# Folding the projection instead of its input, four products at the last frequencies, and an earlier transpose of the next pair in the first four pairs

## The chip, the cores and the metric

The kernel runs on one core of a Trainium2 chip. The metric is the device time of one execution in microseconds (us); lower is better. The core has five engines, each with its own instruction queue that is worked off in order: TensorE (PE; its weight loads are listed apart as PEld), VectorE (DVE), ScalarE (ACT), GpSimd (POOL) and SyncE (SP), which here only issues transfers. PE writes its results to PSUM; DVE and ACT read them there. Engines wait for one another on semaphores.

## The reference

Attention with 4 batches, 8 heads, 768 positions and 64 columns a head; some heads attend to all earlier positions, the others only to the first 4 and the last 64. The result, laid side by side over the heads (768 x 512 for each batch), goes through a gated long convolution:

```python
a = np.exp(scores - max);  a = a / a.sum(-1)          # causal, or causal and (sink or window)
x = (a @ v) laid out as [B, S, 512]
proj = x @ w_proj                                      # 512 -> 3 * 512
x1, x2, x3 = proj in three parts
x2_conv = irfft(rfft(x2, axis=1) * rfft(filter_fft, axis=0), axis=1)
y = x1 * x2_conv * x3
out = y @ w_out
```

## The kernel before

**Attention.** The heads are taken in pairs: 16 pairs n = 0 to 15, four for each batch. For each pair q and k are loaded, cast to bf16 on POOL (`emit_cast`), and transposed to `qkT` (`emit_prep`): for n < 6 by PE, then copied out of PSUM by DVE (q half, L131) and ACT (k half, L133); from n = 6 on by a transposing transfer on SP's queue (L135). The causal blocks of scores are cut into six chunks, two for each third of a pair; `emit_chunks(st, third)` multiplies into PSUM (L318) and takes the exponential on ACT (L325) into `pT`; `emit_masking` multiplies the near blocks by the mask on DVE (L332). `emit_values` (L341, PE) multiplies by v with a column of ones appended, `emit_norm` divides by that column's sum on DVE (L351, L352), and `emit_turn` transposes the result into `xT`: by PE with a DVE copy (L359, L361) for n < 6 and for the last pair of a batch, else by a transfer on SP's queue. POOL also casts v and multiplies it by a mask (`v_aug`, `v_far`).

**Convolution.** The transform over 768 positions is split by even and odd frequencies. For that the sum and the difference of the two halves of the sequence are needed: `emit_fold` makes them from `xT` into `xf`, two operations for each pair, on POOL (128x384 each, L370 and L371), and on DVE for the last pair of a batch. `moe` is a generator for one batch, one `yield` a step: three steps of `x2` (the projection of `xf`, PE L380, then ACT L383); four steps of `X` (the transform by the matrix `G`, PE L254, then ACT): two groups t = 0, 1 with cosine rows and sine rows of 128 frequencies each, and for the last frequencies (t = 2) a tile with 64 cosine and 64 sine rows and once more the same with the rows swapped (`Xs`); the products with the filter's spectrum (`HA`, `HB`) on DVE, `P = X*HA + Xs*HB` (L398, L400, L401); eight steps of `x1` and `x3` (L411, L418, L420); four steps of the inverse transform by `Gi` (six products of 128x384 in each, L427) with ACT and DVE behind it (L430 to L434); three steps of the output product (L440, L443) with a transfer out. `G` is made at the start; `emit_matrix` (POOL) finishes it and `Gi` is its transpose. `setup_steps` transforms the filter in the same manner, also as a generator, in pairs 2 to 4.

**What sets the order.** In pairs 0 to 4 all engines run in the order in which the code is written. From pair 5 on (`MANUAL`) only POOL and SP do; PE, DVE and ACT are put in order by the scheduler at build time, from the same program. `gate_step` takes one step of the generators; a pair from n = 4 on has five such places, so 20 a batch, while `moe` has 22 steps. What is left after pair 15 runs in the tail. PSUM has four buffers of two banks (`bank_pair`) for everything.

## Time and profile before

| | us |
|---|---|
| median of three runs | 253.22 |
| lowest, highest of them | 250.37, 485.48 |
| the profiled execution | 249.91 |
| its span, first to last instruction | 248.2 |

The span has three stages that can be told apart in the trace: a start (0 to about 64 us: setting up, pairs 0 to 4, the filter's transform), a middle (64 to about 200 us: pairs 5 to 15 with the convolution of the batch before woven in) and a tail (200 us to the end: the rest of the third batch's convolution and the whole fourth). PE is busy in 80% of the span, DVE in 66%, ACT in 61%, POOL in 39%.

### The profile page before, as it was taken

The numbers are of one execution on the slowest core, as the hardware profiler recorded it, in microseconds if no ns is written. First come the engines' busy times: TensorE is split into PE (matmuls) and PEld (weight loads), VectorE is DVE, ScalarE is ACT, GpSimd is POOL, SyncE is SP. The second block draws the span as 40 slices with busy tenths as digits, with TensorE's granted clock in tenths as the row PEclk, the third lists the DMA queues.
The fourth block names the chain that finished last, engine by engine and source line by source line (L and its number), as shares of the span: only waits on it lengthen the run. The fifth ranks groups of instructions, "written<-read, shape, count | busy, mean of one in ns | idle before, by whom it ended". The sixth has DMA issues, their size and how long they took to land.

```text
span 248.2 us, 4240 instructions
## 1 busy us (share of the span) xinstructions
PE 197.9 (80%) x1704; PEld 105.0 (42%) x1718; DVE 165.0 (66%) x246; ACT 152.4 (61%) x186; POOL 96.1 (39%) x125
## 2 busy tenths in 40 slices
PE   1533758594899799959997997699899989999880
PEld 0312546252254446523544644353446543455520
DVE  6999588779348964992359749941696593085730
ACT  4956458364479576736897767549896433672431
POOL 5596578772027373470307758420330300000000
PEclk9999995799599999979999999999999999999997
DMA  7999999991031999972899999539211001500015
GB/s 195 301 287 249 288 195 212 198 234 29 0 65 29 213 162 180 219 124 53 262 209 177 216 202 220 98 118 188 45 32 34 4 0 57 196 3 0 0 39 215
DMA packets 89843, 34.42 MB, mean 139 GB/s; under 512 B 80864, under 2 KB 86752, under 8 KB 89824
## 3 DMA queue, kind: packets, MB, share of 16 engines
q1 hardware_dynamic: 86928, 31.28, 57.9%
q0 software_dynamic: 2896, 2.88, 7.1%
q8 instruction: 13, 0.21, 0.4%
q14 instruction: 6, 0.05, 0.1%
HBM read 24.65 MB, written 6.29 MB: 125 GB/s over the span
## 4 chain that ended last, share of the span: by engine, by line
PE 42%; DVE 38%; ACT 12%; issue 3%; DMA 2%; DVEq 0%; ACTq 0%
PE x_ps L411 15%; PE x_ps L380 7%; PE out_ps L440 7%; DVE pT L332 7%; ACT pT L325 6%; PE att L341 5%; PE X_ps L254 5%; DVE attn L352 3%; DVE y L434 3%; DVE conv L432 3%; PE sc L318 3%; DVE qkT L131 2%; DVE P L398 2%; DVE mask L230 2%; DVE conv L433 2%
## 5 line engine op out<-in xcount | busy, mean ns | idle before, releaser
L325 ACT ACTIVATE pT<-sc 128x1024 bf16<-128x1024 f32 x96 | 82.9, 930 | 10.8 <-PE sc L318 10.7
L332 DVE TENSOR_TENSOR pT<-pT,mask 128x1024 bf16<-128x1024 bf16 x48 | 44.0, 917 | 32.7 <-ACT pT L325 32.7
L411 PE MATMUL x_ps<-xT,wproj 128*128 128x384 bf16 x256 | 45.1, 326 | 2.1 <-DVE attn L352 1.5
L318 PE MATMUL sc<-qkT 64*128 64x512 bf16 (+3 forms) x256 | 30.7, 334 | 12.3 <-ACT qkT L133 6.2
L341 PE MATMUL att<-v_aug,pT 128*128 128x65 bf16 x352 | 26.3, 200 | 7.1 <-DVE pT L332 4.2
L411 PEld LDWEIGHTS <-wproj 128*128 128x128 bf16 x256 | 23.7, 98 | 19.2 <-DVE attn L352 3.1
L107 POOL CAST qk_bf<-qk_f 128x768 bf16<-128x768 f32 x31 | 29.7, 985 | 2.7 <-DMA qk_f<-in_k_dram 1.8
L370 POOL TENSOR_TENSOR xf<-xT 128x384 bf16<-128x384 bf16 x12 | 12.6, 1053 | 45.7 <-DMA xT<-attn 38.7
L341 PEld LDWEIGHTS <-pT 128*128 128x128 bf16 x672 | 25.0, 102 | 11.9 <-DVE pT L332 5.1
L440 PE MATMUL out_ps<-wout,y 128*128 128x512 bf16 x91 | 24.1, 394 | 4.2 <-DVE y L434 2.8
L420 DVE TENSOR_TENSOR g<-x1s,x_ps 128x768 bf16<-128x768 bf16 x16 | 15.2, 952 | 16.3 <-PE x_ps L411 16.3
L380 PE MATMUL x_ps<-wproj,xf 128*128 128x512 bf16 x94 | 24.5, 405 | 1.3 <-DVE xf L370 0.9
L318 PEld LDWEIGHTS <-qkT 64*128 64x128 bf16 x256 | 10.4, 98 | 35.3 <-issue 21.5
L254 PE MATMUL X_ps<-x,G 128*128 128x512 bf16 x91 | 22.4, 379 | 1.9 <-DVE attn L352 0.9
L341 PE MATMUL att<-v_far,pT 128*128 128x65 bf16 x320 | 23.1, 200 | 0.0
L418 ACT CAST x1s<-x_ps 128x768 bf16<-128x768 f32 x16 | 12.8, 801 | 14.5 <-PE x_ps L411 14.5
L443 ACT COPY o_sb<-out_ps 128x1024 f32<-128x1024 f32 x12 | 12.2, 1013 | 13.7 <-PE out_ps L440 9.6
L301 POOL MEMSET v_aug<- 128x12 bf16 x16 | 2.4, 150 | 46.4 <-PE att L341 46.4
L398 DVE TENSOR_TENSOR P<-X,HAB 128x1024 bf16<-128x1024 bf16 x12 | 10.2, 847 | 13.0 <-ACT X L389 13.0
L305 POOL TENSOR_TENSOR v_far<-v_aug,vmask 128x520 bf16<-128x520 bf16 x16 | 18.2, 1142 | 1.1
L254 PEld LDWEIGHTS <-G 128*128 128x128 bf16 x120 | 11.4, 100 | 17.2 <-issue 5.4
L427 PE MATMUL c_ps<-Gi,P 128*128 128x384 bf16 x96 | 17.1, 326 | 0.0
(78 smaller groups left out, 250.6 us busy)
## 6 DMA issues: line engine op xcount, KB each, us to landing
qk_f<-in_q_dram SPq DMA_DIRECT2D x16, 384.0 KB, 5.7
qk_f<-in_k_dram SPq DMA_DIRECT2D x16, 384.0 KB, 6.3
v_f<-in_v_dram SPq DMA_DIRECT2D x16, 384.0 KB, 6.8
out_dram<-o_sb SPq DMA_DIRECT2D x12, 512.0 KB, 3.1
wproj<-in_moe_w_proj_dram POOLq DMA_DIRECT2D x3, 512.0 KB, 7.5
filt<-in_moe_filter_fft_dram POOLq DMA_DIRECT2D x1, 768.0 KB, 10.9
wout<-in_moe_w_out_dram POOLq DMA_DIRECT2D x1, 512.0 KB, 7.0
qkT<-qk_bf SPq DMA_TRANSPOSE x10, 3.8
```

The source lines that it names most:

```text
L107: nc.gpsimd.tensor_copy(out=out, in_=in_)
L254: nc.tensor.matmul(ps[:, u, :], lhsT=G[:, m, t, :], rhs=src[:, r, m, :], start=(m == 0), stop=(m == NM - 1))
L305: nc.gpsimd.tensor_mul(v_far, v_aug[:, 0:4], vmask[:, hp, :, :, None].to_broadcast([128, 4, 2, 65]))
L318: nc.tensor.matmul(sc[:, hh, n * 128:(n + cnt) * 128], lhsT=qkT[rows, 1, j * 128:(j + 1) * 128], rhs=qkT[rows, 0, i * 128:(i + cnt) * 128] ...
L325: nc.scalar.activation(out=pT[:, :, c, 0:w], in_=sc[:, :, 0:w], func=AF.Exp, scale=SCALE)
L332: nc.vector.tensor_mul(near, near, kinds)
L341: nc.tensor.matmul(att[:, hh, 65 * i:65 * i + 65], lhsT=st["pT"][:, hh, c, 128 * n:128 * n + 128], rhs=st["v_far" if i >= j + 2 else "v_au ...
L380: nc.tensor.matmul(ps[:, r, :], lhsT=xf[:, cc, r, m * 128:(m + 1) * 128], rhs=wproj[:, cc, DM:2 * DM], start=(cc == 0), stop=(cc == NC - 1))
L411: nc.tensor.matmul(ps[:, s, 0:HS], lhsT=wproj[:, cc, part * DM + cb * 128:part * DM + (cb + 1) * 128], rhs=xT[:, cc, s * HS:s * HS + HS], ...
L420: nc.vector.tensor_mul(g[:, cb, :].rearrange("p (s t) -> p s t", s=2), x1s, halves[1])
L427: nc.tensor.matmul(ps[:, r, 0:HS], lhsT=P[:, t, u, ch], rhs=Gi[:, :, tile_no, :], start=(n == 0), stop=(n == 2))
L440: nc.tensor.matmul(ps[:, n, :], lhsT=y[:, cb, (i + n) * 128:(i + n + 1) * 128], rhs=wout[:, cb, :], start=(cb == 0), stop=(cb == NC - 1))
```

## The change

The projection is made from `xT` itself, for both halves of the sequence, and the sum and difference are taken from its result: ACT copies the product to `x2s`, and DVE adds and subtracts (two operations of 128x512, three times a batch). `emit_fold` and `xf` are gone, with POOL's 24 and DVE's 8 operations.

For the last frequencies the swapped transform is gone (six PE products, one ACT copy and one yield a batch). A new matrix `G2` holds the tile with 64 cosine and 64 sine rows; X of it is multiplied by all four kinds of filter rows at once (one DVE operation of 128x2048 in place of three of 128x1024) into `P[:, 2:4]`, and the inverse transform sums the four products: eight PE products of 128x384 in each of its steps where there were six. `G[4:8]`, now read by the inverse and the filter only, is filled by four POOL copies in place of two, issued in pair 1, not in pair 0.

`qkT` has three buffers, not two. In pairs 0 to 3 the transpose of the next pair stands ahead of the second third of this one, and the mask of the last third has gone to the next pair; pair 4 has its transpose ahead of the first step.

```diff
-        st["qkT"] = qkT = asb.tile([128, 2, S], BF16, name="qkT")
+        st["qkT"] = qkT = asb.tile([128, 2, S], BF16, name="qkT", bufs=3)
...
-        nc.gpsimd.tensor_copy(out=G[:, :, 6:8, 0:64], in_=G[:, :, 4:6, 64:128])
-        nc.gpsimd.tensor_copy(out=G[:, :, 6:8, 64:128], in_=G[:, :, 4:6, 0:64])
+        for part in range(2):
+            for half in range(2):
+                nc.gpsimd.tensor_copy(out=G[:, :, 4 + 2 * part:6 + 2 * part, 64 * half:64 * half + 64],
+                                      in_=G2[:, :, :, 64 * part:64 * part + 64])
...
-            for r in range(2):
+            for half in range(2):
                 for cc in range(NC):
-                    nc.tensor.matmul(ps[:, r, :], lhsT=xf[:, cc, r, m * 128:(m + 1) * 128],
+                    nc.tensor.matmul(ps[:, half, :], lhsT=xT[:, cc, half * HS + m * 128:half * HS + (m + 1) * 128],
...
-            nc.scalar.copy(out=x2[:, :, m, :], in_=ps)
+            x2s = msb2.tile([128, 2, DM], BF16, name="x2s")
+            nc.scalar.copy(out=x2s, in_=ps)
+            nc.vector.tensor_add(x2[:, 0, m, :], x2s[:, 0], x2s[:, 1])
+            nc.vector.tensor_sub(x2[:, 1, m, :], x2s[:, 0], x2s[:, 1])
             yield
...
             if t == 2:
-                Xs = msb2.tile([128, 2, DM], BF16, name="X")
-                ps = emit_forward(x2, ((6, 0), (7, 1)))
-                nc.scalar.copy(out=Xs, in_=ps)
-                yield
-            else:
-                Xs = X[:, ::-1, :]
+                nc.vector.tensor_mul(P[:, 2:4], X[:, None].to_broadcast([128, 2, 2, DM]),
+                                     HAB[:, 2].rearrange("p (a r) c -> p a r c", a=2))
+                continue
...
-                for n, (tile_no, t, u) in enumerate(((2 * r, r, 0), (2 * r + 1, r, 1), (4 + r, 2, r))):
+                for n, (tile_no, t, u) in enumerate(((2 * r, r, 0), (2 * r + 1, r, 1), (4 + r, 2, r), (6 + r, 3, r))):
...
         if n < 4:
+            if last:
+                emit_masking(last, 2)
+            emit_prep(nxt)
             emit_chunks(st, 1)
             if last:
                 emit_values(last)
             emit_masking(st, 0)
             if last:
                 emit_norm(last)
-            emit_prep(nxt)
-            emit_masking(st, 1)
             emit_chunks(st, 2)
-            if last:
-                emit_turn(last)
-                emit_fold(last)
...
-            emit_masking(st, 2)
+            emit_masking(st, 1)
+            if last:
+                emit_turn(last)
```

The order of DVE's queue before, where pair 2 begins (pT_270 and pT_388 are the weights of pairs 1 and 2, attn_421 the result of pair 1, qkT_469 the transposed q of pair 3):

```order
L332 TENSOR_TENSOR pT_270<-pT_270,mask_160 128x2x2x256
L332 TENSOR_TENSOR pT_388<-pT_388,mask_160 128x2x2x256
L351 RECIPROCAL rec_466<-att_422 128x12
L352 TENSOR_TENSOR attn_421<-att_422,rec_466 128x2x6x64
L131 COPY qkT_469<-qkT_ps_470 128x768
```

The same place now (pT_266 and pT_387 are the weights of pairs 1 and 2, qkT_413 the transposed q of pair 3, attn_437 the result of pair 1):

```order
L335 TENSOR_TENSOR pT_266<-pT_266,mask_161 128x2x2x256
L131 COPY qkT_413<-qkT_ps_414 128x768
L335 TENSOR_TENSOR pT_387<-pT_387,mask_161 128x2x2x256
L354 RECIPROCAL rec_482<-att_438 128x12
L355 TENSOR_TENSOR attn_437<-att_438,rec_482 128x2x6x64
```

The copy of the next pair's q has moved ahead of this pair's first mask and of the last pair's division.

ACT's queue before, from the copy of pair 2's k (qkT_350) to that of pair 3's (qkT_469); the sc are the chunks of scores:

```order
L133 COPY qkT_350<-qkT_ps_351 128x768
L325 ACTIVATE pT_270<-sc_367 128x2x512
L325 ACTIVATE pT_270<-sc_371 128x2x256
L325 ACTIVATE pT_388<-sc_389 128x2x512
L325 ACTIVATE pT_388<-sc_393 128x2x512
L325 ACTIVATE pT_388<-sc_413 128x2x512
L325 ACTIVATE pT_388<-sc_417 128x2x384
L133 COPY qkT_469<-qkT_ps_470 128x768
```

And now, from the copy of pair 2's k (qkT_296) to that of pair 3's (qkT_413):

```order
L133 COPY qkT_296<-qkT_ps_297 128x768
L328 ACTIVATE pT_266<-sc_312 128x2x512
L328 ACTIVATE pT_266<-sc_316 128x2x384
L328 ACTIVATE pT_266<-sc_368 128x2x512
L328 ACTIVATE pT_266<-sc_372 128x2x256
L328 ACTIVATE pT_387<-sc_388 128x2x512
L328 ACTIVATE pT_387<-sc_392 128x2x512
L133 COPY qkT_413<-qkT_ps_414 128x768
```

There are six exponentials between two copies in both; the copy stands one third of a pair earlier, behind the first two exponentials of its pair where it stood behind four.

DVE's queue now, at the second batch's projection (x2s are the three copies of it, attn_1503 the result of pair 8, P the first product with the spectrum):

```order
L382 TENSOR_TENSOR x2_1452<-x2s_1499 128x512
L383 TENSOR_TENSOR x2_1452<-x2s_1499 128x512
L354 RECIPROCAL rec_1547<-att_1504 128x12
L355 TENSOR_TENSOR attn_1503<-att_1504,rec_1547 128x2x6x64
L382 TENSOR_TENSOR x2_1452<-x2s_1560 128x512
L383 TENSOR_TENSOR x2_1452<-x2s_1560 128x512
L335 TENSOR_TENSOR pT_1466<-pT_1466,mask_161 128x2x2x256
L395 TENSOR_TENSOR P_1576<-X_1577,HAB_168 128x1024
```

Before, DVE had nothing between PE's projection and PE's transform; now the last add stands behind a division and ahead of a mask and the first product.

57 lines of the change are left out of this document (25 added, 32 removed).

## The prediction, made before the changed kernel had run

> **What bounds the kernel now.** I read the page's head and PE's waits first, then the windows by stage, then the timelines of DVE, ACT and POOL in the start, and last PE's idle gaps in the middle and the tail. In a row of windows stand busy times (and counts) of PE, PEld, DVE, ACT and POOL, PE's granted clock and the DMA engines' share.
>
> ```profile
> span 248.2 us, 4240 instructions
> 0.00:64.00 64.00, 35.38 (x363) 21.54 (x365) 54.34 (x77) 37.16 (x46) 41.63 (x64) 0.90 1.00 212
> 64.00:200.00 136.00, 123.48 (x1142) 64.35 (x1152) 88.89 (x131) 95.42 (x115) 54.44 (x61) 0.97 0.66 130
> 200.00:248.20 48.20, 39.05 (x201) 19.13 (x202) 21.81 (x40) 19.79 (x25) 0.00 (x0) 0.97 0.18 66
> ```
>
> Three stages with different limits. In the middle PE is busy 91% of the time: only PE's work, or one of its rare gaps, counts there. In the start PE works 35 of 64 us and DVE 54: there DVE, and whatever holds it up, sets the pace. In the tail PE works 39 of 48 us.
>
> In the start, these are ACT's and DVE's rows (start, length, engine and line, and in brackets the idle time before and what ended it):
>
> ```profile
> 28.43 0.80 ACT L133 COPY qkT<-qkT_ps 128x768 bf16<-128x768 bf16 x1 [5.88 <-DVE qkT L131]
> 29.13 4.97 ACT L325 ACTIVATE pT<-sc 128x1024 bf16<-128x1024 f32 x6
> 37.09 0.80 ACT L133 COPY qkT<-qkT_ps 128x768 bf16<-128x768 bf16 x1 [2.99 <-DVE qkT L131]
> 46.77 0.80 ACT L133 COPY qkT<-qkT_ps 128x768 bf16<-128x768 bf16 x1 [4.02 <-DVE qkT L131]
> ...
> 23.32 1.28 DVE L332 TENSOR_TENSOR pT<-pT,mask 128x1024 bf16<-128x1024 bf16 x2
> 26.31 0.23 DVE L351 RECIPROCAL rec<-att 128x12 f32<-128x12 f32 x1 [1.71 <-PE att L341]
> 27.45 0.95 DVE L131 COPY qkT<-qkT_ps 128x768 bf16<-128x768 bf16 x1
> 28.32 0.68 DVE L332 TENSOR_TENSOR pT<-pT,mask 128x1024 bf16<-128x1024 bf16 x1
> 28.91 0.55 DVE L361 COPY xT<-xt_ps 128x768 bf16<-128x768 bf16 x1
> 32.51 2.54 DVE L332 TENSOR_TENSOR pT<-pT,mask 128x1024 bf16<-128x1024 bf16 x1 [0.64 <-ACT pT L325]
> 40.45 1.57 DVE L265 TENSOR_TENSOR fold<-filt 128x1536 bf16<-128x1536 bf16 x1
> ```
>
> A pair's pace is the distance of two copies on ACT: 37.09 - 28.43 = 8.66 us, then 46.77 - 37.09 = 9.68, while ACT's own work between them is 0.80 + 4.97 = 5.77. ACT waits each time for DVE's copy of the other half (5.88, 2.99 and 4.02 us, 12.9 together), and that copy stands behind a mask, a reciprocal and a division.
>
> **What POOL does to DVE.** A mask takes 0.60 us undisturbed (28.32 to the next row at 28.91) but 2.54 at 32.51. POOL's rows at that time, and its row of copies in the start:
>
> ```profile
> 16.31 0.51 POOL L240 COPY G<-G 128x384 bf16<-128x384 bf16 x1
> 32.10 1.60 POOL L107 CAST qk_bf<-qk_f 128x768 bf16<-128x768 f32 x2
> 33.68 0.82 POOL L107 CAST v_aug<-v_f 128x768 bf16<-128x768 f32 x1
> ```
>
> POOL's run of casts ends at 33.68 + 0.82 = 34.50, and the mask at 32.51 + 2.54 = 35.05, so 0.55 after it: DVE stood still for 2.54 - 0.60 = 1.94 us. The Trainium skill ("SBUF — State Buffer", section "SBUF: two separate sides") says that GpSimd and two-input VectorE operations exclude each other, and that whoever starts first holds the port for one whole instruction. Exclusion agrees with these rows, the one instruction does not: by that rule the wait would have ended with a cast (0.80 each), and each such wait in the sums below would be about 0.8, not 1.94, which would add some 2 us to the gain, to about 241. I go by the row.
>
> **The start, term by term.** Everything is in the written order here.
>
> (a) The copy for pair 2. Before, it comes at 27.45, behind a wait of 1.71 for PE, reciprocal and division; the masks ahead end at 23.32 + 1.28 = 24.60. Now the division is behind it, and one mask of 0.60 too: 27.45 - 24.60 + 0.60 = 3.45 us earlier. POOL's two G copies (0.51 each), which held DVE at this place, are gone from it: up to 1.0 more. ACT however comes to it with two exponentials fewer done: 4.97 us for 2688 columns are 1.85 ns a column, 896 columns 1.66 us. Net 1.8 to 2.8; I take 2.3.
>
> (b) Pair 2 to pair 3. Now a period is ACT's copy 0.80, four exponentials (1664 columns, 3.08), then DVE's mask 0.60 and copy 0.87 while ACT does two more (1.89): 0.80 + 3.08 + 1.89 = 5.77 undisturbed, with one wait of 1.94 for POOL 0.80 + 3.08 + 0.60 + 1.94 + 0.87 = 7.29, and with POOL's four G copies, now in pair 1 and 4 x 0.51 = 2.0 us long, in the same place 9.3. Against 8.66 that is a gain of 2.9, 1.4, or a loss of 0.6; I take 1.4, since the G copies stand behind a v_far on POOL's queue and may well fall in DVE's PSUM work, which POOL does not stop.
>
> (c) Pair 3 to 4. DVE has the filter's two folds (1.5 each from start to start) ahead of mask and copy: 0.80 + 1.66 for ACT, then 0.60 + 0.5 + 3.0 + 0.60 + 0.87 = 8.0, with a wait for POOL 9.97. Against 9.68: 1.7 or -0.3, I take 0.7.
>
> (d) Pair 4: a mask (0.60) now stands ahead of PE's product with v, against which PE has the filter's transform to do: -0.4, between -0.6 and 0.
>
> Together 2.3 + 1.4 + 0.7 - 0.4 = **-4.0 us**, between 0.3 the other way (1.8 - 0.6 - 0.3 - 0.6) and -7.4.
>
> **The middle.** PE's columns do not change: a batch loses six products of 512 columns and gains eight of 384. What can change are its gaps. These are the largest that the change touches, with what stood in the way:
>
> ```profile
> 64.03 2.32 PE L380 MATMUL x_ps<-wproj,xf 128*128 128x512 bf16 x5 [0.89 <-DVE xf L370]
> 83.34 0.25 PE L341 MATMUL att<-v_aug,pT 128*128 128x65 bf16 x3 [1.23 <-ACT X L394]
> 125.91 2.32 PE L254 MATMUL X_ps<-x,G 128*128 128x512 bf16 x10 [0.45 <-ACT x L383]
> 134.76 2.77 PE L411 MATMUL x_ps<-xT,wproj 128*128 128x384 bf16 x16 [1.53 <-DVE attn L352]
> 132.57 1.26 DVE L398 TENSOR_TENSOR P<-X,HAB 128x1024 bf16<-128x1024 bf16 x1
> 132.07 1.21 POOL L370 TENSOR_TENSOR xf<-xT 128x384 bf16<-128x384 bf16 x1 [9.46 <-DMA xT<-attn]
> L370 POOL TENSOR_TENSOR xf<-xT 128x384 bf16<-128x384 bf16 x12 | 12.6, 1053 | 45.7 <-DMA xT<-attn 38.7
> L389 ACT CAST X<-X_ps 128x1024 bf16<-128x1024 f32 x12 | 12.2, 1024 | 4.5 <-PE X_ps L254 2.6 <-PE att L341 0.9 <-DVE m L400 0.5
> L371 DVE TENSOR_TENSOR xf<-xT 128x384 bf16<-128x384 bf16 x4 | 1.4, 350 | 0.0
> ```
>
> The second X copy goes, and with it the 1.23. DVE's fold goes from the head of the first batch: two operations, 0.6. The product at 132.57 took 1.26 where 0.60 is its undisturbed time, because of POOL's fold at 132.07; the division behind it then held PE 1.53: 0.66 back. One ACT copy (1.02) a batch is gone; around 125 us, where PE waits for ACT, half of it counts in two of three batches, 1.0. Against it each X now waits for ACT's copy and an add: 350 ns for 384 columns are 0.47 for 512, with something queued ahead of it 0.6: 3 x 0.6 = 1.8. Sum -1.23 - 0.6 - 0.66 - 1.0 + 1.8 = **-1.7 us**. DVE's own balance is small, at 0.60 for 1024 columns: per batch 6 adds of 0.33 and one double product of 1.2 against three of 0.60 and two folds of 0.28, +0.8, beside POOL's 24 folds less. Bounds: -3.5 with no wait for the adds, +3 if none of the gaps closes and the adds wait 1.0 each.
>
> qkT's third buffer I cost at nothing:
>
> ```profile
> SPq L135 <- PE sc L318: 45.8, 8, 15.4
> ```
>
> SP's queue waited 45.8 us for PE to be done with a buffer, but no engine ever waited for such a transpose, and the loads behind it are three pairs ahead. If that cover were gone, the transfers xT, which POOL's folds waited for and PE's projection does not yet need, would be late next.
>
> **The tail.** Its PE rows:
>
> ```profile
> 179.90 2.76 PE L254 MATMUL X_ps<-x,G 128*128 128x512 bf16 x12 [0.95 <-DVE attn L352]
> 230.56 4.06 PE L427 MATMUL c_ps<-Gi,P 128*128 128x384 bf16 x24
> 204.55 0.84 PE L440 MATMUL out_ps<-wout,y 128*128 128x512 bf16 x3 [0.77 <-DVE y L434]
> 205.72 0.82 PE L440 MATMUL out_ps<-wout,y 128*128 128x512 bf16 x3 [0.33 <-DVE y L434]
> ```
>
> Six X products at 2.76 / 12 = 0.23 are gone, -1.38. Of the eight inverse products at 4.06 / 24 = 0.17 only the first two count, +0.34, since DVE's sums set the pace of the others. The last add before X (1.0 for ACT, 0.5 for DVE) is covered by six products that PE has ahead of it (1.4). A batch has 21 steps, not 22, so three of the third batch's steps leave the tail for the middle, and the waits of 0.77 and 0.33 for y may find other work: half of them, -0.5. **-1.5 us**, between -2.2 and 0.
>
> **Sum.** 249.91 of the profiled execution - 4.0 - 1.7 - 1.5 = 242.7; I say 243. The runs shown had a median of 253.22 and a lowest of 250.37, so the profiled execution stands at their fast end.
>
> **The rivals.**
>
> 1. The start does not gain: POOL's run of casts and G copies holds DVE in each pair, or the loads do, with DMA at a share of 1.00 over the whole start. Then (a) to (d) give 0 and the rest stands: 249.91 - 3.2 = 246.7, up to 249 if the middle gives nothing. For it speaks the 2.54; against it that no engine waited long for a load in this stage, and that POOL loses six folds there.
>
> 2. Slower: the adds put DVE's queue between two PE works. If the last add of a batch stands behind a reciprocal, a division (0.23 + 0.96) and a mask stopped by POOL (2.54), X waits 3.7 us in each of three batches, and with the middle's gains of 3.5 and a start that gives nothing 249.91 + 11.1 - 3.5 - 1.5 = 256. It decides from about 2.5 us a batch, where it eats all else. The new order has just that division ahead of the second batch's last add; but PE has scores of the pair to do first, and ACT's copy takes 1.0 anyway.
>
> 3. More: the clock. In the start it was granted at 0.90, and the projection's first five products took 2.32 us, 0.46 each, against 0.23 later. If shorter gaps keep the clock up, the 2.3 us of ten such products come back, and with (a) to (d) at their best: 249.91 - 7.4 - 2.3 - 1.7 - 1.5 = 237. The Trainium skill ("TensorE: Matmul & The Clock Gate", section "What's actually happening") makes this a rule: the half clock is the idle state, and a busy window of about 3.4 us releases it. The 0.90 agrees with it; no row here shows that the new gaps are short enough.
>
> **How the numbers follow.** Forecast 0.55, rival 1 0.22, rival 2 0.10, rival 3 0.13. A measurement of this kernel can tell about 2% from no change, 5 us. Rival 3 and most of the forecast (0.48 of 0.55) lie below 247, so 0.61 faster; rival 1 and the forecast's rest, 0.29, are the same; rival 2, 0.10, slower. The range leaves out rival 2 and a little of rival 3: 236 to 251. The forecast's own range is 239 to 247.
>
> **What would show it.** (a) to (c): ACT's waits for DVE qkT (12.9) fall by half, the copies stand 6 to 8 us apart, and x_ps starts near 60, not 64. A mask in the start still over 2 us shows POOL's hold. The middle: no gap at X longer than 1.5, and PE's busy time the same to 1 us. The tail: 24 X products become 18. Wrong would be: x_ps at 64 or later, or gaps of several us before X with an add as their end.

## The result and the profile after

| | before | changed |
|---|---|---|
| median of the runs | 252.93 us (4 runs, one of them 485.48) | 234.58 us (4 runs, 233.42 to 235.46) |
| ratio, 95% interval | | 0.9303 (0.9218 to 0.9389) |
| the same two kernels later, on another chip | 248.59 us (11 runs) | 235.50 us (6 runs); 0.9476 (0.9435 to 0.9517) |
| span of the profiled execution | 248.2 us | 233.7 us |

The kernel became 5 to 7% faster. The changed kernel's time is steady, that of before differs by chip (medians of 247.87 to 252.93), so ratios of different chips can differ by more than their intervals. Ratios compare fast runs alone (a few runs are more than 1.5% above the fastest of their kernel), medians take all runs. The prediction was 243 us with a range of 236 to 251: the direction was right, and the gain was larger than the range allowed.

The head of the changed kernel's page, and its chain of waits:

```profile
span 233.7 us, 4241 instructions
PE 197.0 (84%) x1726; PEld 105.1 (45%) x1726; DVE 157.9 (68%) x254; ACT 148.1 (63%) x182; POOL 70.2 (30%) x103
PE 52%; DVE 28%; ACT 11%; DMA 3%; issue 3%; POOL 0%; SPq 0%; ACTq 0%
```

PE is busy for as long as before (197.0 us, before 197.9), in a span shorter by 14.5. DVE has 7 us less to do and POOL 26. From here on the stages are cut at two events, so that kernels can be compared: the start ends with the first product of the projection that waits for the first batch's last `xT` (x_ps), the middle with the transpose of the last pair (xt_ps). The windows of the stages, first before, then after (columns as in the prediction: PE, PEld, DVE, ACT, POOL, PE's granted clock):

```profile
64.03:198.84 134.81, 122.32 (x1131) 63.51 (x1140) 87.69 (x130) 95.42 (x115) 54.44 (x61) 0.97 0.67 131
```

```profile
0.00:58.75 58.75, 36.60 (x365) 21.68 (x366) 48.68 (x75) 37.39 (x46) 37.83 (x60) 0.94 1.11 238
58.75:188.72 129.97, 122.75 (x1162) 64.74 (x1163) 88.18 (x142) 92.85 (x114) 32.35 (x43) 0.99 0.69 133
188.72:233.70 44.98, 37.64 (x201) 18.70 (x199) 21.06 (x38) 17.82 (x22) 0.00 (x0) 0.96 0.19 70
```

Start 64.0 to 58.8, middle 134.8 to 130.0, tail 49.4 to 45.0: -5.3, -4.8 and -4.4, against the -4.0, -1.7 and -1.5 that were forecast. In the middle PE's busy time is the same (122.32 and 122.75), though it now holds 88 inverse products where it held 48, and 54 of X where it held 72 (68 of them recorded); its idle time fell from 134.81 - 122.32 = 12.5 us to 7.2. The view of PE's waits, in the middle alone (us in total, how often, the longest), says which; its main lines, before:

```profile
PE xt_ps L359 <- DVE attn L352: 3.0, 3, 1.5
PE x_ps L411 <- DVE attn L352: 1.5, 1, 1.5
PE sc L318 <- DVE conv L433: 1.5, 2, 1.0
PE att L341 <- ACT X L394: 1.2, 1, 1.2
PE out_ps L440 <- ACT pT L325: 1.1, 1, 1.1
PE X_ps L254 <- DVE attn L352: 0.9, 1, 0.9
```

and after:

```profile
PE x_ps L377 <- DVE xT L364: 1.6, 1, 1.6
PE x_ps L377 <- DVE attn L355: 1.4, 1, 1.4
PE X_ps L257 <- DVE attn L355: 1.4, 1, 1.4
PE xt_ps L362 <- DVE attn L355: 1.3, 2, 0.8
PE X_ps L257 <- DVE x L382: 0.8, 1, 0.8
PE out_ps L437 <- DVE y L431: 0.6, 1, 0.6
PE x_ps L408 <- DVE attn L355: 0.4, 1, 0.4
```

The first line of the second list, 1.6, is the gap with which the middle begins, and lies ahead of it. The waits for a division (attn) before the transposes fell from 3.0 to 1.3 and that at x1's and x3's x_ps (L411, now L408) from 1.5 to 0.4, but that at X_ps rose from 0.9 to 1.4, and there is a new one of 1.4 at the projection (L377): together 5.4 before and 4.5 now. What went are the waits at sc (1.5 for conv), at att for the copy of X (1.2) and at out_ps for ACT (1.1); the new wait for the adds (x) is 0.8 in all. How far DVE is held up shows in the group of its masks, in the middle alone (count, then busy time and mean ns of one), before and after:

```profile
L332 DVE TENSOR_TENSOR pT<-pT,mask 128x1024 bf16<-128x1024 bf16 x34 | 27.8, 818 | 28.4 <-ACT pT L325 28.4
```

```profile
L335 DVE TENSOR_TENSOR pT<-pT,mask 128x1024 bf16<-128x1024 bf16 x34 | 23.4, 689 | 21.7 <-ACT pT L328 21.7
```

The same 34 operations take 129 ns less each. In the start, the copies of k on ACT, which mark a pair's pace:

```profile
24.30 0.80 ACT L133 COPY qkT<-qkT_ps 128x768 bf16<-128x768 bf16 x1 [2.24 <-DVE qkT L131]
31.20 0.80 ACT L133 COPY qkT<-qkT_ps 128x768 bf16<-128x768 bf16 x1 [0.81 <-DVE qkT L131]
40.17 0.80 ACT L133 COPY qkT<-qkT_ps 128x768 bf16<-128x768 bf16 x1 [3.20 <-DVE qkT L131]
```

The periods are 6.90 and 8.97 us (before 8.66 and 9.68), the waits for DVE's half 6.25 us together (before 12.9).

### The profile page after: what moved, and what is told of

Same layout as the page of the kernel before. It is cut to its first block, busy times and chain, and to the rows that moved or that the text cites. A ratio compares the mean times of both kernels' runs of the same rounds, so it can differ in the third digit from the quotient of the medians.

```text
span 233.7 us, 4241 instructions
## 1 busy us (share of the span) xinstructions
PE 197.0 (84%) x1726; PEld 105.1 (45%) x1726; DVE 157.9 (68%) x254; ACT 148.1 (63%) x182; POOL 70.2 (30%) x103
## 4 chain that ended last, share of the span: by engine, by line
PE 52%; DVE 28%; ACT 11%; DMA 3%; issue 3%; POOL 0%; SPq 0%; ACTq 0%
PE x_ps L408 17%; PE att L344 7%; PE x_ps L377 6%; PE out_ps L437 6%; PE X_ps L257 6%; ACT pT L328 5%; PE sc L321 5%; DVE pT L335 4%; DVE attn L355 4%; DVE y L431 3%; PE c_ps L424 3%; DVE conv L429 3%; DVE conv L430 2%; DMA qk_f<-in_k_dram 2%; DVE x L383 2%
## 5 line engine op out<-in xcount | busy, mean ns | idle before, releaser
L335 DVE TENSOR_TENSOR pT<-pT,mask 128x1024 bf16<-128x1024 bf16 x48 | 36.8, 769 | 21.7 <-ACT pT L328 21.7
L408 PE MATMUL x_ps<-xT,wproj 128*128 128x384 bf16 x256 | 45.3, 326 | 1.0 <-ACT x1s L415 0.4
L408 PEld LDWEIGHTS <-wproj 128*128 128x128 bf16 x256 | 23.9, 98 | 18.2 <-issue 2.2
L107 POOL CAST qk_bf<-qk_f 128x768 bf16<-128x768 f32 x31 | 27.6, 913 | 5.5 <-DMA qk_f<-in_k_dram 4.5
L377 PE MATMUL x_ps<-wproj,xT 128*128 128x512 bf16 x96 | 24.0, 395 | 3.3 <-DVE xT L364 1.6
L437 PE MATMUL out_ps<-wout,y 128*128 128x512 bf16 x96 | 22.7, 380 | 1.2 <-DVE y L431 1.1
L424 PE MATMUL c_ps<-Gi,P 128*128 128x384 bf16 x128 | 22.8, 326 | 0.2 <-DVE conv L430 0.2
L321 PEld LDWEIGHTS <-qkT 64*128 64x128 bf16 x256 | 9.6, 98 | 29.7 <-issue 24.4
L415 ACT CAST x1s<-x_ps 128x768 bf16<-128x768 f32 x16 | 12.9, 806 | 11.6 <-PE x_ps L408 11.6
L257 PE MATMUL X_ps<-x,G 128*128 128x512 bf16 x72 | 17.2, 379 | 2.5 <-DVE attn L355 1.4
L381 ACT CAST x2s<-x_ps 128x1024 bf16<-128x1024 f32 x12 | 12.3, 1024 | 11.0 <-PE x_ps L377 8.3
L382 DVE TENSOR_TENSOR x<-x2s 128x512 bf16<-128x512 bf16 x12 | 7.0, 584 | 14.3 <-ACT x2s L381 14.3
L389 ACT CAST X<-X_ps 128x1024 bf16<-128x1024 f32 x12 | 11.9, 1019 | 6.3 <-PE X_ps L257 5.8
```

Of the source, the lines that this page charges most:

```text
L107: nc.gpsimd.tensor_copy(out=out, in_=in_)
L257: nc.tensor.matmul(ps[:, u, :], lhsT=matrix[:, m, t, :], rhs=src[:, r, m, :], start=(m == 0), stop=(m == NM - 1))
L321: nc.tensor.matmul(sc[:, hh, n * 128:(n + cnt) * 128], lhsT=qkT[rows, 1, j * 128:(j + 1) * 128], rhs=qkT[rows, 0, i * 128:(i + cnt) * 128] ...
L335: nc.vector.tensor_mul(near, near, kinds)
L377: nc.tensor.matmul(ps[:, half, :], lhsT=xT[:, cc, half * HS + m * 128:half * HS + (m + 1) * 128], rhs=wproj[:, cc, DM:2 * DM], start=(cc = ...
L408: nc.tensor.matmul(ps[:, s, 0:HS], lhsT=wproj[:, cc, part * DM + cb * 128:part * DM + (cb + 1) * 128], rhs=xT[:, cc, s * HS:s * HS + HS], ...
```

## The experiments

In this table ratios are to the kernel before on the same chip, and stages are those of the profiled execution.

| kernel | start | middle | tail | median us | ratio, 95% |
|---|---|---|---|---|---|
| before | 64.0 | 134.8 | 49.4 | 252.93 | 1 |
| changed | 58.8 | 130.0 | 45.0 | 234.58 | 0.9303 (0.9218, 0.9389) |
| e17 changed, again | 57.8 | 131.1 | 45.1 | 235.50 | 0.9476 (0.9435, 0.9517) |
| e1 order alone | 60.2 | 136.7 | 49.3 | 247.64 | 0.9935 (0.9886, 0.9983) |
| e2 fold alone | 57.3 | 133.9 | 49.4 | 241.45 | 0.9705 (0.9612, 0.9798) |
| e3 fold alone, no adds | 60.1 | 130.4 | 49.4 | 240.78 | 0.9676 (0.9598, 0.9754) |
| e8 changed, old order | 58.6 | 128.5 | 45.0 | 233.70 | 0.9366 (0.9247, 0.9486) |
| e4 POOL reads xT again | 60.9 | 145.2 | 45.0 | 251.46 | 1.0127 (1.0081, 1.0172) |
| e5 POOL, other data | 60.7 | 133.2 | 45.1 | 240.70 | 0.9639 (0.9533, 0.9746) |
| e6 POOL waits only | 58.6 | 137.7 | 45.0 | 240.10 | 0.9615 (0.9498, 0.9732) |
| e13 POOL reads xT, later | 60.8 | 132.9 | 45.0 | 240.25 | 0.9683 (0.9634, 0.9731) |
| e7 one step more | 58.5 | 129.6 | 49.4 | 237.86 | 0.9544 (0.9433, 0.9655) |
| e11 one step less | 57.5 | 136.7 | 39.9 | 236.24 | 0.9486 (0.9433, 0.9538) |
| e9 old last frequencies | 56.5 | 135.7 | 49.5 | 243.59 | 0.9795 (0.9734, 0.9855) |
| e14 e9 with 21 steps | 59.1 | 135.7 | 46.1 | 242.46 | 0.9783 (0.9734, 0.9831) |
| e15 e14, no swapped transform | 60.1 | 131.7 | 44.7 | 237.22 | 0.9587 (0.9546, 0.9627) |
| e16 three operations on DVE | 56.9 | 132.1 | 45.0 | 236.99 | 0.9546 (0.9502, 0.9590) |
| e10 two qkT | 56.9 | 130.7 | 45.1 | 236.03 | 0.9472 (0.9415, 0.9530) |
| e12 three o_sb | 56.8 | 132.1 | 43.9 | 235.51 | 0.9477 (0.9413, 0.9540) |

The start took 56.5 to 60.1 us in kernels that hardly differ there (e9, e7, e15, e16, e17 and others), at a granted clock of 0.82 to 0.97: 2 us in the start of one profile mean nothing. With the same steps and work the tail repeats to 0.1; the middle was 130.0, 131.1, 130.7 and 132.1 in four kernels that do the same work there (the changed one, e17, e10, e12), so that 2 us of it mean nothing either.

**e1, the order alone.** The kernel before, with the new written order of pairs 0 to 4 (`G`'s copies in pair 1 are part of it) and no more:

```diff
         if n < 4:
+            if last:
+                emit_masking(last, 2)
+            emit_prep(nxt)
             emit_chunks(st, 1)
...
-            emit_prep(nxt)
-            emit_masking(st, 1)
             emit_chunks(st, 2)
```

> The kernel before with the new written order of pairs 0 to 4 alone (and the G copies in pair 1); folds, four groups of X and two qkT buffers stay. Theory P (three places, each with its own part of the change: start 5.3 us by the order, middle and tail by the folds and the four products): the first full row of x_ps near 59 to 60, in place of 64.0, time about 5 us under before, ratio 0.98. Theory Q (all of it is POOL's folds, which stop DVE everywhere): the order alone gains under 2 us, since the folds still stop the masks: ratio 0.995. Theory S (the woven steps set it): nothing past the start, same as P here.

The start shrank by 3.8 us and the time by 0.65%, 1.6 us; the middle was 1.9 longer. The order does by itself what it was forecast to do in the start, and the kernel hardly gains from it.

**e2, the fold on the projection alone.** The kernel before without POOL's and DVE's folds, with the adds behind the projection:

```diff
-        engine = nc.vector if st["pair"][1] == HP - 1 else nc.gpsimd
-        halves = st["xT"][:, st["pair"][1], 0:HS], st["xT"][:, st["pair"][1], HS:S]
-        engine.tensor_add(st["xf"][:, st["pair"][1], 0, :], *halves)
-        engine.tensor_sub(st["xf"][:, st["pair"][1], 1, :], *halves)
+        return
...
-            nc.scalar.copy(out=x2[:, :, m, :], in_=ps)
+            x2s = msb2.tile([128, 2, DM], BF16, name="x2s")
+            nc.scalar.copy(out=x2s, in_=ps)
+            nc.vector.tensor_add(x2[:, 0, m, :], x2s[:, 0], x2s[:, 1])
+            nc.vector.tensor_sub(x2[:, 1, m, :], x2s[:, 0], x2s[:, 1])
```

> The kernel before with the projection made from xT and the add and subtract on DVE behind it, no folds; the order, the four groups of X and 22 steps stay. P: DVE stopped less often, the gaps of PE at 107 to 110 us and 134 us close; about -5 us, ratio 0.98, start unchanged but for about 1 us. Q: nearly all of the 14.5 us, ratio 0.95. S: no more than 1 us, since steps and PE's columns are as before, ratio 0.995.

3% faster, without the new order: this part carries what the order alone did not. In the profile it lies in the start, 57.3 us against 64.0; the middle (133.9) is 0.9 shorter, which one profile cannot tell from nothing, and PE's waits for divisions in it are 7.8 us in all, against 5.4 before. The copies of k on ACT in its start:

```profile
28.54 0.80 ACT L133 COPY qkT<-qkT_ps 128x768 bf16<-128x768 bf16 x1 [5.72 <-DVE qkT L131]
35.34 0.80 ACT L133 COPY qkT<-qkT_ps 128x768 bf16<-128x768 bf16 x1 [1.14 <-DVE qkT L131]
43.87 0.80 ACT L133 COPY qkT<-qkT_ps 128x768 bf16<-128x768 bf16 x1 [2.86 <-DVE qkT L131]
```

The periods are 6.80 and 8.53 us with the old order; e1, which keeps the folds and has the new one, has 6.90 and 9.54.

**e3, the same without the adds.** ACT copies straight into `x2`; DVE has nothing to do there:

```diff
-            x2s = msb2.tile([128, 2, DM], BF16, name="x2s")
-            nc.scalar.copy(out=x2s, in_=ps)
-            nc.vector.tensor_add(x2[:, 0, m, :], x2s[:, 0], x2s[:, 1])
-            nc.vector.tensor_sub(x2[:, 1, m, :], x2s[:, 0], x2s[:, 1])
+            nc.scalar.copy(out=x2[:, :, m, :], in_=ps)
```

> As the run with the fold's place alone, but the sum and the difference are left out altogether (x2 is the plain projection of the two halves), so what the adds cost is the difference of the two. P: the adds cost 0.5 to 2 us; so -6 to -7 us against before. Q: the same as with the adds, as only POOL matters. My prediction put the waits for the adds at 1.8.

0.9676 against 0.9705, inside both intervals, 0.7 us by the medians: the runs tell what the 24 adds are worth neither from nothing nor from the 1.8 us that the forecast had charged for waiting for them. (In the two profiles the middle without them is 3.5 us shorter and the start 2.8 longer.)

**e8, the changed kernel with the old order.**

```diff
         if n < 4:
-            if last:
-                emit_masking(last, 2)
-            emit_prep(nxt)
             emit_chunks(st, 1)
...
+            emit_prep(nxt)
+            emit_masking(st, 1)
             emit_chunks(st, 2)
```

> The changed kernel with the written order of pairs 0 to 4 as before. The order alone moved the start by 3.9 us but the time by 1.6 only, and the folds alone moved the start by up to 6.8. P: +4 to +5, 239, start back at 63 to 64. Overlap (theory O: folds and order take away the same waits in the start): +1 to +2, 236, start at 58 to 60.

No slower than the changed kernel (233.70 and 234.58 us), with the same start (58.6). The periods of ACT's copies are 6.81 and 8.10 us, like those of e2. So in the start order and fold take away the same waits, those of ACT for DVE's copy, and the one that comes second gains nothing that these runs show.

**e4, POOL reads xT again.** The changed kernel with POOL's 24 operations in the places of the old folds, into a tile that nobody reads:

```diff
+    spare = const.tile([128, 2, HS], BF16, name="spare")
+
+    def emit_fold(st):
+        if st["pair"][1] == HP - 1:
+            return
+        halves = st["xT"][:, st["pair"][1], 0:HS], st["xT"][:, st["pair"][1], HS:S]
+        nc.gpsimd.tensor_add(spare[:, 0, :], *halves)
+        nc.gpsimd.tensor_sub(spare[:, 1, :], *halves)
```

> The changed kernel with POOL's 24 operations put back where they stood, reading the same halves of xT, but writing a spare tile that nobody reads: POOL's time and its hold on DVE come back, no dependence does. P: 3 to 5 us slower than the changed kernel, about 238.5. Q: 8 us or more slower, about 243. S, or if it was the folds' latency and not their hold: within 1 us of the changed kernel, about 235.

251.46 us: by the medians 16.9 more than the changed kernel, though no engine waits for these results. Nearly all lies in the middle, 145.2 against 130.0. PE, DVE and ACT work in the same order as in the changed kernel, and so does POOL but for the 24 operations; the gaps alone are new. DVE's rows (start, length) in the stretch ahead of a long one:

```profile
129.59 1.39 DVE L407 TENSOR_TENSOR m<-X,HAB 128x1024 bf16<-128x1024 bf16 x1
130.91 1.30 DVE L405 TENSOR_TENSOR P<-X,HAB 128x1024 bf16<-128x1024 bf16 x1
132.14 1.31 DVE L408 TENSOR_TENSOR P<-P,m 128x1024 bf16<-128x1024 bf16 x1
133.37 0.68 DVE L335 TENSOR_TENSOR pT<-pT,mask 128x1024 bf16<-128x1024 bf16 x1
...
136.94 1.54 DVE L335 TENSOR_TENSOR pT<-pT,mask 128x1024 bf16<-128x1024 bf16 x1
138.39 0.22 DVE L354 RECIPROCAL rec<-att 128x12 f32<-128x12 f32 x1
138.65 0.96 DVE L355 TENSOR_TENSOR attn<-att,rec 128x768 bf16<-128x768 f32 x1
```

and POOL's at the time, the first of them the second operation of a pair whose first began at 128.21, after a wait of 4.32 us for `xT`:

```profile
129.08 1.36 POOL L378 TENSOR_TENSOR spare<-xT 128x384 bf16<-128x384 bf16 x1
130.39 2.51 POOL L107 CAST qk_bf<-qk_f 128x768 bf16<-128x768 f32 x2
135.47 0.15 POOL L304 MEMSET v_aug<- 128x12 bf16 x1 [2.57 <-PE att L344]
135.51 0.95 POOL L107 CAST v_aug<-v_f 128x768 bf16<-128x768 f32 x1
136.55 1.38 POOL L308 TENSOR_TENSOR v_far<-v_aug,vmask 128x520 bf16<-128x520 bf16 x1
```

Each of the products, sums and masks shown that meets a busy POOL takes 1.3 to 1.5 us; the mask at 133.37, while POOL waits, takes 0.68. The division comes late, and PE stands for it (the bracket is the idle time before the row); the windows row of the next 4 us has PE's clock as the third figure from the end:

```profile
139.66 4.31 PE L418 MATMUL x_ps<-xT,wproj 128*128 128x384 bf16 x16 [2.47 <-DVE attn L355]
139.66:143.66 4.00, 4.00 (x16) 1.87 (x16) 1.41 (x2) 0.80 (x1) 1.22 (x2) 0.63 0.66 127
```

Such 16 products take 2.77 at the full clock (the row at 134.76 in the prediction): the gap costs 2.47 and then 1.54 more. Over the whole middle DVE is busy for 99.7 us, where the same operations take 88.2 in the changed kernel.

**e5, e6 and e13: hold and wait apart.** In e5 the same operations read the masks, which are there all the time, so that POOL never waits for them. In e6 POOL waits for `xT`, but has only two columns to add:

```diff
-        halves = st["xT"][:, st["pair"][1], 0:HS], st["xT"][:, st["pair"][1], HS:S]
+        halves = mask[:, 0, 0:2].rearrange("p k c -> p (k c)")[:, 0:HS], mask[:, 1, 0:2].rearrange("p k c -> p (k c)")[:, 0:HS]
```

```diff
-        nc.gpsimd.tensor_add(spare[:, 0, :], *halves)
-        nc.gpsimd.tensor_sub(spare[:, 1, :], *halves)
+        nc.gpsimd.tensor_add(spare[:, 0, 0:2], halves[0][:, 0:2], halves[1][:, HS - 2:HS])
```

> The changed kernel with the same 24 POOL operations of 128x384 at the same places, reading the mask table (there since the start) instead of xT: POOL works as long, and waits for nothing. If it is the hold on DVE while POOL works (theory H), as slow as with xT, about 250; if it is POOL standing still until xT has been transposed, so that its casts behind come late or all at once (theory W), within 2 us of the changed kernel, 234 to 237. Between: both.

> The changed kernel with POOL waiting for xT at the same places, but with one operation of 128x2 in place of two of 128x384: nearly no POOL time, the whole wait. H: 234 to 237, as the changed kernel. W: about 250. Between: the parts of the two runs should add up to the 16.9 us of both together.

240.70 and 240.10 us: 6.1 and 5.5 more than the changed kernel, 11.6 together, where both at once cost 16.9. (The profiled execution of e6 took 243.03, the longest of its four by 2.9, so its middle in the table is long too.) Either half is dear, and together they are dearer than their sum. That left open whether it was the wait on top of the work, or that POOL reads just this tile. e13 tells it: e4's operations on `xT`, but from pair 6 on one pair later, when `xT` should be there:

```diff
-        if hp == 0:
-            emit_fold(last)
+        if n >= 6:
+            emit_fold(state[n - 2])
...
-        if hp != 0:
-            emit_fold(last)
```

> The changed kernel with the same POOL operations on xT as in the run where POOL reads xT again (same size, same number, nobody reads the result), but from pair 6 on each pair's two operations stand one pair later on POOL's queue, when xT has long arrived, so that POOL does not wait there. Theory W (the cost is POOL's wait, which bunches the casts behind it on top of DVE's work): it falls to about what the same operations on other data cost, 240 us, ratio 0.96 (0.95 to 0.975), middle 133 to 135 us. Theory R (reading xT itself is dear, because PE and the transfers use that tile at the time): it stays near 250 us, ratio 1.00 to 1.015, middle 142 us or more.

240.25 us, middle 132.9: theory W. Of the nine places in the middle, POOL finds `xT` there at the first six; at the last three it still waits, 21.2 us in all, where e4 waits 37.7 at nine. With the first six waits gone the same reads cost what other data cost. The masks in the middle, for e4 and for e13:

```profile
L335 DVE TENSOR_TENSOR pT<-pT,mask 128x1024 bf16<-128x1024 bf16 x34 | 27.4, 805 | 21.9 <-ACT pT L328 21.9
```

```profile
L335 DVE TENSOR_TENSOR pT<-pT,mask 128x1024 bf16<-128x1024 bf16 x34 | 24.8, 730 | 20.4 <-ACT pT L328 20.4
```

DVE's busy time in the middle goes with the cost: 88.2 us in the changed kernel, 91.8 in e13, 93.4 in e6, 95.3 in e5 and 99.7 in e4, for the same operations in the same order. The rows above show how it comes about at one place: a POOL that has waited for `xT` works off its folds and the casts behind them without a pause, and meets DVE where DVE has its own run of two-input operations. That the other gaps come about likewise was not traced one by one.

**e7 and e11, a step more and a step less.** e7 adds one `yield` a batch to the changed kernel, 22 steps as before; e11 takes one away (20 steps), by putting the second and third group of X into one:

```diff
+                yield
                 continue
```

```diff
             nc.scalar.copy(out=X, in_=ps)
-            yield
+            if t != 1:
+                yield
```

> The changed kernel with a yield put back in at the last group of X, so that a batch has 22 steps again and three more of them are left for the tail. Theory P': the tail was 49.4 us in every run with 22 steps and 45.0 in both with 21, so the steps are its cause: tail back to about 48.5, and the middle shorter by the work that leaves it (2 to 3 us): time +1 to +2, ratio to the changed kernel 1.005. If it is the missing X products and waits themselves: tail stays at 45 to 46.

> The changed kernel with the second and third group of X in one step, so that a batch has 20 steps, as many as four pairs take, and all but the last of the third batch's steps leave the tail. Theory S: the middle takes the three steps (8 inverse products and 16 output products, 4.9 us of PE) nearly for free: tail 39 to 41, middle up by 0 to 3, time 230 to 232. If the middle is bound by PE (my prediction): tail shorter by 5, middle longer by 5, time as the changed kernel, 234.5.

The tail is 49.4 us at 22 steps, 45.0 at 21, 39.9 at 20. The middle is 129.6, 130.0, 136.7. The windows of the middle, of e7 and then of e11:

```profile
58.51:188.07 129.56, 120.43 (x1129) 63.00 (x1138) 85.70 (x137) 92.01 (x112) 32.75 (x43) 0.98 0.73 134
```

```profile
57.50:194.20 136.70, 129.08 (x1185) 66.92 (x1186) 94.62 (x149) 95.16 (x117) 31.23 (x43) 0.98 0.68 129
```

PE idles 9.1 us in the middle with 22 steps, 7.2 with 21, 7.6 with 20. From 22 to 21, PE takes 2.3 us more work into a middle that grows by 0.4. From 21 to 20 it takes 6.3 more and the middle grows by 6.7: there was no more room, and the time stayed (236.24).

**e9, e14, e15, e16: the four products.** e9 is the changed kernel with the swapped transform, three DVE products and six inverse products put back; e14 is e9 less its additional `yield`; e15 is e14 less the swapped transform, and so leaves out six X products and one copy a batch without the two more inverse products a step that the changed kernel has in their place; e16 is the changed kernel with three DVE operations in place of one.

```diff
-                nc.vector.tensor_mul(P[:, 2:4], X[:, None].to_broadcast([128, 2, 2, DM]),
-                                     HAB[:, 2].rearrange("p (a r) c -> p a r c", a=2))
-                continue
+                Xs = msb2.tile([128, 2, DM], BF16, name="X")
+                ps = emit_forward(x2, ((6, 0), (7, 1)))
+                nc.scalar.copy(out=Xs, in_=ps)
+                yield
```

```diff
-                Xs = msb2.tile([128, 2, DM], BF16, name="X")
-                ps = emit_forward(x2, ((6, 0), (7, 1)))
-                nc.scalar.copy(out=Xs, in_=ps)
+                Xs = X[:, ::-1, :]
```

```diff
-                nc.vector.tensor_mul(P[:, 2:4], X[:, None].to_broadcast([128, 2, 2, DM]),
-                                     HAB[:, 2].rearrange("p (a r) c -> p a r c", a=2))
+                four = HAB[:, 2].rearrange("p (a r) c -> p a r c", a=2)
+                m3 = msb2.tile([128, 2, DM], BF16, name="m2")
+                nc.vector.tensor_mul(P[:, 2], X, four[:, 0])
+                nc.vector.tensor_mul(m3, X, four[:, 1])
+                nc.vector.tensor_mul(P[:, 3], X, four[:, 1])
```

> The changed kernel with the swapped transform back: four groups of X, six inverse products a step, 22 steps. The run with one more step alone had a tail of 49.4 us against 45.0 and was 3.3 us slower. If the four products are worth only the step (theory S), the same: 237 to 239, tail 49.4. If the X products, the ACT copy and the DVE operations are worth something in the middle too (my prediction: 1.2 for PE's wait on the copy, 1.0 for the copy), 2 to 3 us more: 240 to 241.

> The changed kernel with the swapped transform, three DVE products and six inverse products a step put back as they were before, but without the additional step (21 a batch, as in the changed kernel). Theory S (the four products gained by the step they save): tail 45 us, time as the changed kernel plus 1 us of PE's work or less, ratio 0.93 to 0.945. Theory P (they gained because the swapped transform, its copy on ACT and the products behind it stand ahead of the division in DVE's queue): tail 45 us, but the middle stays near 135 us, ratio 0.955 to 0.97.

> As the run before, but the swapped transform and its copy on ACT are left out, and the last frequencies are multiplied with the rows as they stand: the result at these frequencies is left wrong by that. 21 steps, three DVE operations of 1024 columns (not one of 2048), six inverse products a step. Theory A (the swapped transform and ACT's copy are what cost in the middle): 130 us in the middle, ratio 0.92 to 0.935. Theory D (DVE's three operations against one are what cost): middle 133 us or more, ratio 0.945 or more.

> The changed kernel with the one DVE operation of 2048 columns at the last frequencies split into three of 1024 (two products and one of them once more, which nobody reads); PE's and ACT's work and the 21 steps are those of the changed kernel. Theory D (DVE's third operation and the two starts cost in the middle): middle 131.5 to 133 us, ratio 0.01 above the changed kernel's on the same chip. Theory A (DVE's part is not what costs): middle 129.5 to 130.5 us, no difference to the changed kernel within the intervals.

> The changed kernel itself, as the mark for the run beside it and for the two runs with the old work of the last frequencies: ratio 0.93 to 0.947, middle 130 us, tail 45 us.

By the medians: e9 243.59, e14 242.46, e15 237.22, the changed kernel 235.50 (e17). The windows of the middle, of e9, e14 and e15:

```profile
56.50:192.22 135.72, 124.42 (x1139) 63.34 (x1140) 88.82 (x143) 95.09 (x115) 32.74 (x43) 0.96 0.72 130
59.10:194.77 135.67, 124.54 (x1149) 64.48 (x1158) 92.46 (x147) 95.77 (x118) 31.91 (x43) 0.98 0.67 127
60.12:191.79 131.67, 119.07 (x1132) 62.44 (x1140) 91.79 (x147) 92.93 (x115) 33.73 (x43) 0.99 0.69 131
```

e14's middle stayed at 135.7, as theory P has it, and its ratio, 0.978, lies above P's range (0.955 to 0.97). e15 falls between its theories, with the middle near A's and the ratio within D's. e16's ratio bears out D, with 0.007 where 0.01 was said; its middle, 132.1, lies in D's range, but so does that of e12, which has the changed kernel's work there.

The step by itself, with the old work, gives 3.4 us in the tail of one profile and nothing that the ratios can tell (0.9795 and 0.9783). The swapped transform and its copy are worth 5.2 us (e14 to e15, with the same chip), 4.0 of it in the middle. This is PE's own work and its clock, not a gap that closed: PE's busy time in the middle falls by 5.5 us, and its idle time rises from 11.1 to 12.6. In e16, which has the inverse products in place of the X products, PE is busy for 3.7 us more than in e15 (122.75) and idle for 9.4, and the time is no longer (236.99, on another chip; ratios 0.9587 and 0.9546): the added products fill idle time. DVE's three operations against one are worth 1.5 us (e16 against e17, on one chip, runs of 235.73 to 238.14 against 234.63 to 235.70); the intervals of the two ratios overlap.

Two pairs of kernels price the whole of this part. e9 and e7 have 22 steps each and differ in it alone: the middle is 135.7 and 129.6, the tail 49.5 and 49.4. On one chip, e9 took 243.59 and e10 (the changed kernel but for one `qkT` buffer, below) 236.03: the four products and the step together are worth 7.6 us there, and order and folds the rest, a ratio of 0.9795 or 5 us. What shows where such work hurts is one place of e14, the transposes of a pair, with the windows row of the 10 us around it, and the like stretch of the changed kernel:

```profile
150.02 0.51 PE L359 MATMUL xt_ps<-identity,attn 128*128 128x128 bf16 x6 [1.88 <-DVE attn L352]
149.10:159.10 10.00, 9.03 (x44) 3.40 (x46) 4.02 (x7) 4.91 (x6) 1.45 (x2) 0.83 0.54 122
```

```profile
148.75:158.75 10.00, 9.52 (x89) 4.42 (x87) 3.54 (x6) 8.13 (x10) 2.02 (x3) 1.00 0.43 159
```

PE waited 1.88 for a division and then worked at 0.83 of the clock over these 10 us, where the changed kernel has 1.00. As in e4, a late division costs twice.

**e10 and e12, the buffers.** e10 is the changed kernel with two `qkT` buffers; e12 has three for the output copy `o_sb` besides (with two for `qkT`, for the room):

```diff
-        st["qkT"] = qkT = asb.tile([128, 2, S], BF16, name="qkT", bufs=3)
+        st["qkT"] = qkT = asb.tile([128, 2, S], BF16, name="qkT")
```

```diff
-            o_sb = msb2.tile([128, 2, DM], FP32, name="o_sb")
+            o_sb = msb2.tile([128, 2, DM], FP32, name="o_sb", bufs=3)
```

> The changed kernel with two qkT buffers. My prediction costed the third at nothing: 234 to 235.5, within 1 us of the changed kernel. A rival: the loads behind the transposes on SP's queue come late: 2 us or more slower.

> The changed kernel with three buffers for the output's copies, and two qkT buffers to make room. At the end ACT waits 1.86 us for the first transfer of the batch before its last copy: without that wait the end comes 1.5 to 1.9 us earlier, 232.8. If the transfers then share the DMA engines so that the last one ends no earlier: 234.5.

The third `qkT` buffer gives nothing (0.9472, the changed kernel 0.9476). The third `o_sb` makes the tail 1.1 us shorter (43.9) and the time no shorter (235.51). The two show how much luck is in one profile: at the same place, after the same gap, PE's clock held in the one and fell in the other (e10, then e12):

```profile
126.32 2.77 PE L408 MATMUL x_ps<-xT,wproj 128*128 128x384 bf16 x16 [2.47 <-DVE attn L355]
```

```profile
124.80 4.45 PE L408 MATMUL x_ps<-xT,wproj 128*128 128x384 bf16 x16 [2.47 <-DVE attn L355]
```

No kernel was measurably faster than the changed one.

## Why the prediction fell short

**The start, (a) to (d): right in size, wrong in its cause.** -4.0 was forecast, -5.3 came. The periods came as worked out: 6.90 for (b) where 7.29 was forecast, 8.97 for (c) where the sum gave 9.0, and the copy for pair 2 at 24.30, 4.1 earlier or 2.5 net of ACT's two exponentials (2.3 forecast). But the sum took these for the order's work, to which the rest is added, and had no term for the six folds of POOL that leave the start; only its first rival names them. e2, with the old order and no folds, has a start of 57.3 and periods of 6.80 and 8.53. e1 shows the order to be worth 1.6 us of the time by itself, and e8 shows no gain from it once POOL's folds are gone. The two parts remove the same waits and don't add up; that the sum of the order alone met the start's size is partly luck, since one profile's start varies by 2 us. (The weakest case, 1.8 - 0.6 - 0.3 - 0.6, is a gain of 0.3, not a loss.)

**The middle: the step that failed.** "In the middle PE is busy 91% of the time: only PE's work, or one of its rare gaps, counts there" was true, and PE's busy time is indeed unchanged. The terms that failed are those of the last frequencies: -1.23 for PE's wait on the copy of X and -1.0 for half a copy in two batches, together -2.2. Measured, from e9 to e7, the middle loses 6.2 us: 4.0 of PE's busy time and 2.2 of its idle time. "PE's columns do not change" holds for the whole kernel and not for this stage: the middle of e7 has 18 X products of 512 columns less and 16 inverse products of 384 more than that of e9, 3072 columns or six X products, by the 0.23 of the prediction an estimated 1.4 us; the rest of the busy time goes with the clock, 0.96 in e9 and 0.98 in e7. Of the idle time the sum had the copy's gap alone, while PE's waits for divisions are 8.3 us in e9 and 4.9 in e7. How much of these is luck stays open: the four kernels with the changed kernel's work in the middle have 4.5 to 6.6, and the 5.4 of the kernel before lie in that range.

**POOL's folds: a term without a price.** They were put down as "beside POOL's 24 folds less". e2 gives the price of taking them from the kernel before, 3%; but its profile, shorter by 7.6 us, has 6.7 of that in the start and 0.9 in the middle. e9, without folds, has masks of 711 ns in the middle, where the kernel before has 818, and its middle is 135.7, no shorter: masks that take less time do not shorten that stage by themselves. e4's 16.9 is the price of such operations in the changed kernel, and not what taking them out has gained.

**The two halves of the change, on one chip** (e9 and e10 beside the kernel before): order and folds were forecast at -4.0 - 0.6 - 0.66 + 1.8 = -3.5 and gave some 5; the last frequencies and the step at -1.23 - 1.0 - 1.5 = -3.7 and gave 7.6. So most of what is missing from the forecast is in the second half.

**The adds.** +1.8 was charged; e3 can tell it neither from nothing nor from 1.8, and the wait for them that the profile names in the middle is 0.8 (X_ps for x) in all. The rival that rested on them, 256 us, fell by its own condition: it needed 2.5 us a batch, and the longest wait for an add was 0.8.

**The last frequencies, part by part.** The transform and its copy gave 5.2 us (e14 to e15), DVE's operations 1.5 (e16 against e17), and the inverse products in place of the X products cost nothing that shows (e15 to e16). The mechanism of the forecast, that ACT's copy stands ahead of what PE waits for, is not what e15 shows: PE's idle time in the middle grew without it, and PE's own work fell.

**The tail: a term mis-sized.** "Three of the third batch's steps leave the tail for the middle", half of the waits for y, -0.5. It was to be the smaller part of the tail, and it is nearly all: with a step more (e7) the tail is 49.4, as before the change. That tail has six X products less and 16 inverse products more than that of the kernel before, so that the -1.38 + 0.34 of the forecast do not show. A step less gave 4.4 from e7 to the changed kernel and 3.3 from e9 to e14. The forecast priced the waits that the steps might fill and not the steps, which are PE's work taken out of a stage where PE has idle time (41.29 us of PE's work in the 49.4 of e7's tail, 37.64 in 45.0 here). In the middle that takes them in, idle time fell from 9.1 to 7.2 and the stage grew by 0.4.

**qkT's third buffer** was rightly costed at nothing (e10).

**The clock** (the third rival, 237 us): it lay nearest to the time. It was meant for the start, where the products at x_ps still run slow (2.00 for five, before 2.32) and the clock went from 0.90 to 0.94. In the middle, which the rival did not speak of, the clock went from 0.97 to 0.99; by these rounded figures that is an estimated 134.81 x 0.03 - 129.97 x 0.01 = 2.7 us of a full clock. How much of the gain is the clock's own cannot be told from the gaps', since one follows the other; no run holds the clock and keeps the gaps.

What stays open: why e5's operations, which wait for nothing, still cost 6 us, is told by DVE's held operations only as far as the profile shows their lengths (95.3 us busy in the middle for 88.2); no run moved POOL's work to where DVE has no two-input operation. And why POOL's operations cost so much in the middle of the changed kernel, while taking the folds out of the kernel before shortened its middle so little, no run tells.

## What to carry to other kernels

An operation off the critical path is not free when its engine stops another: look at the lengths of the other engine's operations (here 818 ns for a mask that needs 600), summed over the stage, and at which waits that other engine ends; then price it by a run, for with masks of 711 ns and no folds the middle stayed as long. When a change has parts, make a kernel with one part put back, and compare on one chip: here it showed the part that had been priced at 3.7 us to give 7.6. That columns stay the same over a kernel does not say that they stay the same in each stage. An in-order queue that waits for a late transfer and then works off its backlog can do it at the worst time; here the same work one pair later cost 11 us less. Where work is cut into steps that fill another stage, count the steps that are left at the end: each one saved is PE's work out of the tail, until the stage that takes it has no idle time left.

## What the runs showed of the hardware

**The clock falls after short gaps.** Over the 19 profiles (both kernels and the experiments), in the middle, PE's granted clock in the 4 us behind a gap of PE: of 47 gaps of 1.0 to 1.8 us (without the one that the stage begins with), 4 were followed by a clock below 0.99 (all in the kernel before and in e1, each with another gap of 1.0 us or more at most 4 us away); of 8 gaps of 1.8 to 2.0 us, 3; of 6 gaps of 2.4 to 2.7 us, 5, at 0.57 to 0.65; of 2 above 3 us, both, at 0.50 and 0.62. The gap with which the middle begins is another matter: it is 1.1 to 1.6 us in 16 profiles, and 12 of these show a clock of 0.50 to 0.64 behind it. In all 12 PE has two more gaps of 0.7 to 1.0 us in the 5 us before; so it has in e12, where the clock held. It held in e1, e2 and e3 too, with a gap of 1.1 behind one of 1.7 (e1) or of 1.0. So short gaps close together mostly go with a low clock too. The Trainium skill ("TensorE: Matmul & The Clock Gate", section "What's actually happening") puts the half clock behind at least one idle window of about 3.4 us, windows that run freely; the runs show it behind single gaps from 1.9 us on in part and from 2.5 us on nearly always, and behind less where gaps stand close together. This is seen in the profiles, not isolated by a run of its own.

**How long POOL holds DVE.** In e4 the two engines alternate: DVE's operations of 0.60 take 1.30 while POOL's two casts of 0.80 take 2.51. That fits a hold of one instruction at a time, as the Trainium skill has it ("SBUF — State Buffer", section "SBUF: two separate sides"); the mask of 2.54 in the prediction, which ended only behind the last of three casts, does not. Both occur, and what decides between them was not tried.
